# VectorE's program in a two-trip loop of three skippable parts, the first trip only branching over them

## The chip, the cores and the metric

One core of one Trainium2 chip. The time is the device time of one execution in microseconds; each kernel is run several times, and medians are quoted. The profile is of one execution; its times count from the start of the span, which is 1.8 us shorter than the device time of that same execution (294.18 us for the kernel before).

A ratio with an interval is the mean time of one kernel's fast runs over the mean time of the kernel before's fast runs in the same rounds, so it is not quite the ratio of the medians.

## The reference, cut to what matters

```python
h  = x + attention(layernorm(x), k_cache, v_cache, wq, wo)   # one token, B=2, 32 heads of 192,
                                                             # the last 2048 of 8192 positions
h2 = h + (gelu(layernorm(h) @ w_gate) * (layernorm(h) @ w_up)) @ w_down
```

Nearly all the work is reading: 122.29 MB of keys, values and weights, each byte used once.

## The kernel before: the parts that the change and the argument touch

The kernel records every operation in a list for its engine, with the semaphores it waits for, and then writes the lists out. TensorE's list is written as a four-trip loop; the other engines' lists are straight lines:

```python
    def emit(self, name, eng, sems, ops=None):
        for o in self.per.get(name, ()) if ops is None else ops:
            self.emit_one(o, eng, sems, [...])
    ...
        @block.vector
        def _(e):
            P.emit("dve", e, sems)
```

VectorE's list has 290 operations, 318 instructions when built: first some 55 that build constants (identity, masks, the normalised x), then the copies of transposed keys and the softmax of 16 groups, then the FFN's small steps.

All loads go through one queue into a ring of six slots of 24,576 bytes in each partition. A load is issued when what it overwrites has been read. The first four (k0, wq, k1, v0) need nothing; the fifth, k2, overwrites part of wq:

```python
K_AT = (0, SLOT, 3 * SLOT, 5 * SLOT)
V_AT = (2 * SLOT, 4 * SLOT)
WQ_AT = 3 * SLOT + SLOT // 2          # 2.5 slots long
...
        transposes(0, 0); transposes(0, 1)   # k0: TensorE, copied out by ScalarE and VectorE
        q_rows()                             # reads wq, then frees it: k2 may be issued
```

## Time and profile before

| | before |
|---|---|
| time, median (range) | 293.96 us (293.91 to 294.05) |
| span in the profile | 292.4 us |
| mean DMA rate over the span | 418 GB/s |
| busy share: TensorE, VectorE | 67%, 44% |
| VectorE's first operation | 1.10 us |
| packets of instructions on q14 in the span | 3 |

How to read it: the DMA engines are the bound, as the prediction shows with the profile's rows (one queue of data holds 97.9% of their time). The page counts 16 DMA engines, and the semaphore of each load is raised 16 times. I take that for 16 parts, one on each engine: wq has 128 pieces of 2.27 us, 8 of them make 18.1 us, and wq's first part landed 18.13 us after k0's. What waits for a load starts after the last of the 16: wq's came at 29.73 us, the query matmuls start at 29.87. The trace keeps the 16 times, though not which DMA engine is which. For the kernel before (us; the three latest of 16 in columns four to six):

```
load  issued   first   14th    15th    last     last behind first
k0      0.74   10.50   10.70   10.71   10.82    0.3
wq      1.42   28.63   28.83   28.92   29.73    1.1
v0      2.63   43.21   43.53   44.35   44.85    1.6
k2     35.65   50.53   50.83   51.67   52.15    1.6
k13   188.12  220.41  222.03  222.05  222.51    2.1
wd2   260.85  287.07  288.65  288.66  289.09    2.0
```

Even here a few parts are late, and the lateness hardly shrinks (0.1 us at most): the pieces of a load are of equal size and the DMA row stands at nine tenths or more from the fifth slice to the last but one, so a part that is 1.10 us behind in wq is still 1.14 behind in v0 and in k2, and 1.13 in k5.

The 16 landings also hint at what made them late, by the time at which each one falls behind. TensorE's packets on q8 (16,384 bytes) at 34.70, 51.09, 60.18, 77.56 and 92.17 us each put one more part 1.6 us behind: one part is so in k1, five are in k5. So TensorE's fetches fall on different parts. VectorE's two packets on q14, at 17.06 and 149.81, fit one and the same part: it is 1.1 behind from wq on (the second latest in v0) and 2.1 from v7 on.

### The profile page before, as it was taken

To read this page: it belongs to the slowest core of one execution; us is meant where nothing else is said; L and a number is where in the kernel's file an instruction comes from. 1 tells how busy PE (TensorE), PEld (TensorE's weight loads), DVE (VectorE), ACT (ScalarE), POOL (GpSimd) and SP (SyncE) were. 2 spreads that over 40 slices of the span, in tenths; PEclk is the share of its full clock that TensorE was granted. 3 is DMA by queue.
4 is the path that set the end of the run, shared out by engine and by line. 5 is a ranking of instruction groups with operands and counts; after the bars stand their busy time and mean duration, and the time that the engine had idled before them with its cause. 6 is when DMAs were issued, how large, how long until landed. Compare 5 with 4: busy or idle time off the path is not lost.

```text
span 292.4 us, 5066 instructions
## 1 busy us (share of the span) xinstructions
PE 196.2 (67%) x2141; PEld 151.6 (52%) x2141; DVE 128.2 (44%) x311; ACT 96.3 (33%) x120; POOL 8.6 (3%) x36
## 2 busy tenths in 40 slices
PE   2450769848677298849493597659596959585584
PEld 1440436728475285628281575456566657563242
DVE  5950075713447045525264155425265535352231
ACT  2150116623442143616161154325342525341000
POOL 4000020000000000000000000000000000000000
PEclk9996679995979579998899599969797968897755
DMA  7997999999999999999999999999999999999993
GB/s 269 430 531 338 433 447 436 430 433 430 423 408 448 430 434 428 430 430 430 430 402 450 434 430 430 430 430 434 430 430 430 430 430 434 430 430 405 425 416 148
DMA packets 6362, 122.44 MB, mean 419 GB/s; under 512 B 718, under 2 KB 848, under 8 KB 1360
## 3 DMA queue, kind: packets, MB, share of 16 engines
q1 hardware_dynamic: 6336, 122.29, 97.9%
q8 instruction: 7, 0.11, 0.2%
q14 instruction: 3, 0.02, 0.0%
q10 hardware_dynamic: 16, 0.01, 0.0%
HBM read 122.29 MB, written 0.00 MB: 418 GB/s over the span
## 4 chain that ended last, share of the span: by engine, by line
DMA 76%; PE 20%; SPq 2%; DVE 1%; issue 0%
DMA ring<-in_A_k_cache_dram 57%; PE tps L555 15%; DMA ring<-in_A_wq_dram 10%; DMA ring<-in_B_w_down_dram 10%; PE tps L576 2%; SPq L347 2%; PE ops L657 1%; PE m L708 1%; PE m L690 1%; DVE ktr L567 0%; DVE ering L408 0%; PE m L850 0%; PE m L641 0%; PE m L671 0%; DVE yrow L856 0%
## 5 line engine op out<-in xcount | busy, mean ns | idle before, releaser
L555 PE MATMUL tps<-identf,ring 128*128 128x128 f32 x768 | 114.4, 317 | 45.4 <-DMA ring<-in_A_k_cache_dram 44.1
L555 PEld LDWEIGHTS tps<-identf,ring 128*128 128x128 f32 x768 | 105.5, 166 | 48.4 <-DMA ring<-in_A_k_cache_dram 45.4
L564 ACT ACTIVATE ktr<-tps 128x1024 bf16<-128x1024 bf16 x80 | 79.4, 1023 | 84.0 <-PE tps L555 84.0
L567 DVE COPY ktr<-tps 128x1024 bf16<-128x1024 bf16 x112 | 74.0, 687 | 71.3 <-PE tps L555 70.4
L632 ACT ACTIVATE eexp<-sm,nm 128x512 bf16<-128x512 f32 x16 | 11.5, 721 | 64.1 <-DVE nm L630 64.1
L657 PE MATMUL ops<-ring,ering 128*32 128x384 bf16 x512 | 24.7, 337 | 4.8 <-DMA ring<-in_A_v_cache_dram 4.7
L613 PE MATMUL sps<-ktr,rq 128*16 128x512 bf16 x384 | 25.8, 403 | 1.1 <-POOL rq L408 1.1
L621 DVE CUSTOM_DVE_ANT_1 sm<-sps,mska 128x512 f32<-128x512 f32 x16 | 11.1, 692 | 34.9 <-PE sps L613 34.9
L657 PEld LDWEIGHTS ops<-ring,ering 128*32 128x32 bf16 x512 | 12.7, 98 | 13.3 <-DMA ring<-in_A_v_cache_dram 6.2
L613 PEld LDWEIGHTS sps<-ktr,rq 128*16 128x16 bf16 x384 | 9.5, 90 | 11.9 <-issue 2.1
L628 PEld LDWEIGHTS m<-mrhs,pm 128*128 128x128 bf16 x16 | 1.5, 96 | 22.8 <-DVE mrhs L404 22.8
L576 PE MATMUL tps<-ring,xnT 128*32 128x384 bf16 x80 | 5.7, 472 | 10.9 <-DMA ring<-in_A_wq_dram 10.9
L628 PE MATMUL m<-mrhs,pm 128*128 128x16 bf16 x16 | 2.9, 183 | 14.7 <-DVE mrhs L404 14.7
L408 POOL TENSOR_TENSOR rq<-qs,mask 128x96 bf16<-128x96 bf16 x16 | 5.6, 359 | 195.4 <-PE sps L613 161.3
L576 PEld LDWEIGHTS tps<-ring,xnT 128*32 128x32 bf16 x80 | 3.1, 134 | 13.4 <-issue 11.1
L599 DVE CAST qs<-ops 128x384 bf16<-128x384 f32 x1 | 0.6, 558 | 17.7 <-PE ops L594 17.7
L408 DVE TENSOR_TENSOR ering<-m,mask 128x256 bf16<-128x256 f32 x16 | 6.7, 419 | 3.2 <-PE m L641 3.2
L708 PE MATMUL m<-ring,ot 128*2 128x320 bf16 x96 | 4.7, 340 | 2.4 <-DMA ring<-in_A_wo_dram 2.4
L583 ACT ACTIVATE qrow<-tps 128x768 bf16<-128x768 f32 x1 | 0.8, 812 | 15.6 <-PE tps L576 15.6
L788 ACT ACTIVATE lnv<-tps,eps_t 98x1 f32<-98x1 f32 x1 | 0.3, 262 | 17.3 <-PE tps L786 17.3
L641 PE MATMUL m<-sel,eexp 128*128 128x64 bf16 x64 | 5.0, 206 | 1.2 <-ACT eexp L632 1.2
L641 PEld LDWEIGHTS m<-sel,eexp 128*128 128x128 bf16 x64 | 4.7, 111 | 1.7 <-DVE nm L630 1.3
(124 smaller groups left out, 88.8 us busy)
## 6 DMA issues: line engine op xcount, KB each, us to landing
ring<-in_A_k_cache_dram SPq DMA_DIRECT2D x16, 3072.0 KB, 31.2
ring<-in_A_v_cache_dram SPq DMA_DIRECT2D x16, 3072.0 KB, 27.3
ring<-in_A_wq_dram SPq DMA_DIRECT2D x1, 7680.0 KB, 28.3
ring<-in_A_wo_dram SPq DMA_DIRECT2D x4, 1920.0 KB, 21.5
ring<-in_B_w_gate_dram SPq DMA_DIRECT2D x1, 1920.0 KB, 31.5
ring<-in_B_w_up_dram SPq DMA_DIRECT2D x1, 1536.0 KB, 24.8
ring<-in_B_w_down_dram SPq DMA_DIRECT2D x1, 960.0 KB, 27.2
ring<-in_B_w_down_dram SPq DMA_DIRECT2D x1, 480.0 KB, 27.9
```

Source lines behind the costliest of these rows:

```text
L347: P.op("sp", lambda e, v=v, src=src: e.dma_start(v, src), W=toks + [("sem", sem)], dma=sem)
L408: return lambda e: e.tensor_tensor(out=out, in0=a, in1=b, op=op)
L555: ins = e.transpose(tps[bi][:, 128 * u:128 * (u + 1)], kv[:, off:off + 128], identf[:, :])
L564: act(lambda e, dst=dst, bv=bv: e.activation(out=dst, in_=bv, func=ACT.Copy), W=[("kt", n)], X=[("t", bi)])
L567: dve(lambda e, dst=dst, bv=bv: e.tensor_copy(dst, bv), W=[("kt", n)], X=[("t", bi)], cls=0)
L576: ins = e.matmul(tps[0][32 * r:32 * (r + 1), 0:384], lhsT=xnT[:, c, 32 * J:32 * (J + 1)], rhs=wq[:, c, 1536 * J + 384 * r:1536 * J + 384 * ...
L613: ins = e.matmul(sps[32 * ch:32 * ch + 16, :], lhsT=rq[:, g % 4, k, :], rhs=ktr[:, k // 2, 1024 * ch + k % 2:1024 * (ch + 1):2], start=(k ...
L621: dve(lambda e: e.tensor_tensor_reduce(out=sm[:, :].rearrange("p (u x) -> p u x", u=4), in0=sps[:, :].rearrange("p (u x) -> p u x", u=4), ...
L632: act(lambda e: e.activation(out=eexp[:, :], in_=sm[:, :], func=ACT.Exp, bias=nm[:, 0:1], scale=1.0, accum_out=zr[:, g % 4:g % 4 + 1]), R= ...
L641: ins = e.matmul(o, lhsT=eexp[:, 128 * u:128 * (u + 1)], rhs=sel64[:, :], start=True, stop=True)
L657: ins = e.matmul(ops_[32 * r:32 * (r + 1), 0:384], lhsT=ering[:, g % 4, t, :], rhs=vv[:, 384 * t:384 * (t + 1)], start=(g % 4 == 0 and t < 4),
L708: ins = e.matmul(m1[32 * r:32 * r + 2, 192:512], lhsT=ot[:, kk, :], rhs=wo[:, kk - k0, 320 * h:320 * (h + 1)], start=(kk == 1 or J < 2 and ...
```

## The change

Intent: let VectorE touch its whole program once at the start, so that its instructions are on the chip when they are needed.

```diff
+DVE_CUTS = (80, 200)
 ...
         @block.vector
         def _(e):
-            P.emit("dve", e, sems)
+            l = P.per["dve"]
+            with e.Fori(0, 2) as i:
+                for lo, hi in zip((0,) + DVE_CUTS, DVE_CUTS + (len(l),)):
+                    with e.If(i > 0):
+                        P.emit("dve", e, sems, l[lo:hi])
```

In the built program the branches stand at instruction 4, 86 and 218, and the loop's end at 321 and 322 of 325.

## The prediction

> **What bounds the kernel now.** I read the page's slices first, then the DMA queue's table, then the chain that ended last, then the timelines of TensorE and of the DMA-issuing engine at the start, where the change acts.

> The slices show the 16 DMA engines at nine tenths or more in nearly every slice, while VectorE is at four tenths on average:

> ```profile
> DVE  5950075713447045525264155425265535352231
> ...
> DMA  7997999999999999999999999999999999999993
> ```

> The queue table says that one queue of data holds 97.9% of the engines' time. The two rows marked "instruction" are the fetches of the engines' own programs, 7 and 3 in the whole span:

> ```profile
> q1 hardware_dynamic: 6336, 122.29, 97.9%
> q8 instruction: 7, 0.11, 0.2%
> q14 instruction: 3, 0.02, 0.0%
> ```

> The chain that ended last is 76% DMA and 1% VectorE. So the kernel is a stream of 122.29 MB at about 430 GB/s, and the question about any delay is whether it leaves that stream without work. The head of the chain in order of time (start, length, what) shows where it could:

> ```profile
> 1.42 28.31 DMA ring<-in_A_wq_dram
> 29.73 0.14 issue
> 29.87 5.76 PE tps L576 x61
> 35.64 0.02 issue
> 35.65 0.54 SPq L347
> ```

> Four loads are issued in the first 3.2 us (k0, wq, k1, v0). The fifth, k2, overwrites part of wq and is issued at 35.65, when the query matmuls (L576) have read wq. TensorE's timeline at the start (start, length, what, idle before):

> ```profile
> 3.75 0.35 PE L468 MATMUL m<-identb,xrow 2*128 2x2 bf16 x5 [3.75 <-DVE eps_t L439]
> ...
> 10.86 3.54 PE L555 MATMUL tps<-identf,ring 128*128 128x128 f32 x16 [4.26 <-DMA ring<-in_A_k_cache_dram]
> 15.07 3.89 PE L555 MATMUL tps<-identf,ring 128*128 128x128 f32 x32 [0.67 <-DVE ktr L567]
> 29.87 5.74 PE L576 MATMUL tps<-ring,xnT 128*32 128x384 bf16 x80 [10.91 <-DMA ring<-in_A_wq_dram]
> ```

> The k0 transposes end at 18.96, and TensorE then has nothing to do for **10.91 us** until wq has landed. VectorE feeds it three things before that: the identity (written by 3.43 us in VectorE's timeline), the normalised x (7.43) and the copies of the transposed k0, which stand behind 13 us of constant building (first copy 14.34).

> [...]the packets on q14 are 8,192 bytes[...]; TensorE's on q8 are 16,384. Two of q14's, at 17.05 and 149.81 us, fit VectorE[...] (59 and 179 of its instructions had started[...]).[...] In this trace TensorE's compare-and-branch records, which it already has in its four-trip loop, last 68 to 349 ns, and each of its three jumps back to the loop's top is followed by the next instruction within 0.3 us: there the target was still on the chip (no q8 fetch falls between 92 and 275 us).[...] the q14 fetch at 17.05 ran while wq moved (10.8 to 28.6 us), among its 61,440-byte pieces of 2.27 us each, not after them.

> **The change part by part.** Nothing is removed. No engine but VectorE has a different order, and VectorE executes the same operations with the same waits. Added on VectorE:

> - *Trip one.* Two register moves, three taken branches over the parts, one register add, one taken branch back. In the built program the branches stand at instruction 4, 86, 218 and about 322 of some 325. Branches alone, at TensorE's 0.07 to 0.35 us: 4 times 0.2 is 0.8 us. Fetches: with block borders near 61, 189 and 317 (from the two fetches above, a few instructions uncertain), the jump to 86 lands in the second block, which must be preloaded since the kernel before walks into it without a pause; the jump to 218 lands in the third[...]; the jump to 322 lands at or just beyond the fourth border; the jump back needs the first block, which may have been overwritten. That is one to three misses.
> - *Cost of a miss.* No row measures it. The nearest small transfer is xrow (2.5 KB): issued at 0.74, landed at 2.27, so 1.5 us; the output store took from 290.26 to 291.98, 1.7 us. With the 24,576-byte pieces of k0 in the way (0.91 us each) I estimate 2 to 3 us. So VectorE starts D = 0.8 + 2 x 2.2, about **5 us late**, between 2 and 10.
> - *Trip two.* Three branches not taken and the loop's end: under 1 us in all, spread over the run, and partly under waits for other engines (VectorE waits 70.4 us in total for the transposes alone).

> What of D reaches the end? With D = 5 the identity is there at 8.4, before k0 lands at 10.8. Constant building ends at 19.4 instead of 14.4, the k0 copies about 24.4, the transposes about 24, still 5 us before wq lands at 29.73. D costs nothing up to 10.9. Beyond that k2 would be issued late, but k1 and v0 are still queued at 35.65: the trace has v0's last semaphore at 44.85, so less some 1.5 us of start-up, another **7.5 us** pass before the stream runs dry. Only D over about 18 us costs time, and then one for one. In mid-run, loads are issued far ahead (one at 36.88 lands 29.88 us later, while its own 3,145,728 bytes at 430 GB/s need 7.3), so a stall of VectorE of a few us there is absorbed too. Sum: 293.94 + 0 at the start + 0 in the middle + about 0.1 for branches in the tail = **294.0 us**.

> **The rivals.** *A, a miss in the tail.* The last VectorE operations are moved some 5 instructions later, so that the fourth block's border may fall among them (the gelu at 284 to 288 us). There the slack is small: the last weights land at 289.09 and the matmuls ahead of them (L850) end at 288.93. If trip one spoils sequential prefetch, a miss there costs about 2 us: 296.[...] Against: 190 instructions stand ahead in straight order on trip two[...]. I give it one in ten. *B, fetches stuck behind whole packets.* [...]for k0 (8 pieces per engine, 7.3 us) and wq (18 us), two misses could take 25 us, D would pass 18 and the time go to 300 or more.[...] Against: it was still served inside wq. Three in a hundred. *C, faster.* Trip one could act as a warm-up that takes fetch stalls out of the run. But the waits of VectorE are all named after another engine's work, with no unexplained gap at 17 or 150 us, and VectorE does not bound the stream. One in a hundred.

> **Range and chances.** The centre is 294.0; the three runs before spread by 0.14 us. Low 293.4 for a rearrangement of the stream; high 296.2 for rival A. 2% is 5.9 us, which only rival B reaches: slower 0.03, faster 0.01, same 0.96.

> **What would show it.** VectorE's first operation starts about 5 us later than 1.10, and q14 shows two to four more fetches in the first 10 us (right), or none (the misses were not there, D about 1). TensorE's idle time before L576 shrinks from 10.91 to about 6 and is still ended by wq; L576 still starts near 29.87 and the fifth load near 35.65. From there every time in the chain agrees within 0.3 us. The prediction is wrong if L576 is released by VectorE, if the DMA row shows a dip near slice 6, or if VectorE has an unexplained gap after 284 us.

Passages are cut from this record where that is marked: they stated what no trace or run of this case shows. That a fetch waits for all pieces of a load on its DMA engine was B's assumption (the "whole packets" of its heading are these pieces; its 25 us are my estimate from 8 pieces of k0 at 0.91 us and 8 of wq at 2.27). In "it was still served inside wq" the fetch at 17.05 us is meant. The block borders near 61, 189 and 317, and with them the one to three misses, are an estimate from the two fetches at which 59 and 179 of VectorE's instructions had started, 120 apart; that the borders were set 128 apart was not shown by the trace.

## The result and the profile after

The changed kernel takes **299.11 us** (298.97 to 299.16) against 293.96: ratio 1.0174, interval 1.0156 to 1.0192. That is 5.15 us slower, within 2% but well outside the range of 293.4 to 296.2.

The page's slices and queue table of the changed kernel:

```profile
DVE  0006738563526335616237154434366425262231
...
DMA  7998989999999999999999999999999999999990
...
q1 hardware_dynamic: 6336, 122.29, 96.5%
q8 instruction: 7, 0.11, 0.2%
q14 instruction: 9, 0.07, 0.1%
```

VectorE does nothing in the first two slices and almost nothing in the third, and q14 has 9 packets instead of 3. Their share of the DMA engines' time is 0.1%, which looks like nothing. The data still moves in every slice, though slice 6 shows 8 tenths instead of 9, the dip that the prediction had named as a sign of being wrong.

VectorE's timeline (start, length, operation, idle before it):

```profile
21.74 0.23 DVE L436 CAST cf<-ci 128x128 f32<-128x128 int32 x1 [21.74 <-issue]
...
33.25 1.26 DVE L568 COPY ktr<-tps 128x1024 bf16<-128x1024 bf16 x2
```

Its first operation starts at 21.74 us, 20.6 later than before, and "issue" says that it waited for no other engine. TensorE's timeline:

```profile
25.38 3.65 PE L556 MATMUL tps<-identf,ring 128*128 128x128 f32 x16
33.98 5.56 PE L556 MATMUL tps<-identf,ring 128*128 128x128 f32 x32 [4.95 <-DVE ktr L568]
39.48 3.43 PE L577 MATMUL tps<-ring,xnT 128*32 128x384 bf16 x80
```

The query matmuls (here L577) start at 39.48 instead of 29.87, straight after the k0 transposes. The idle 10.91 us are used up. The chain that ended last, in order of time:

```profile
12.07 9.49 issue
...
33.98 5.56 PE tps L556 x32
39.55 3.39 PE tps L577 x80
42.95 0.54 SPq L348
...
44.24 26.62 DMA ring<-in_A_k_cache_dram
```

So k2 is issued at 42.95 instead of 35.65. From this chain the loss looks like VectorE's late start. But a chain only says that a load was issued at 44.24 and landed 26.62 us later, not why it took as long. The landings of the changed kernel:

```
load  issued   first   14th    15th    last     last behind first     last, against before
k0      0.74   10.49   10.70   10.74   12.33    1.8                   +1.5
wq      1.42   28.63   28.80   28.86   33.41    4.8                   +3.7
v0      2.63   43.25   43.39   43.44   48.96    5.7                   +4.1
k2     42.95   52.56   52.80   52.91   56.26    3.7                   +4.1
k13   192.68  222.40  224.11  224.12  227.05    4.7                   +4.5
wd2   265.42  289.03  290.71  290.72  293.60    4.6                   +4.5
```

Fifteen parts of wq land when they did before. **One part is 4.8 us late**, and stays late. By v0, which was issued at 2.63 us as before, 4.1 of the 5 us are already lost, and no load had yet been issued late. When k2 is late, the other fifteen DMA engines wait 2.0 us for it (50.53 becomes 52.56), but the late one does not: its k2 follows its v0 by 56.26 - 48.96 = 7.3 us, the ordinary time of a load (8 pieces of 0.91 us).

The packets on q14 fit. The trace has the times of the 8,192-byte packets of instructions in the span:

```
before   17.06                                      113.16  149.81
after     4.59  9.98  16.40  19.64  25.15  33.84    117.04  147.98  293.56
```

The one at 113 to 117 us I take for ScalarE's, since it came at 97.82 in the run delay_only below, where ScalarE has six instructions more. That leaves VectorE 2 before and 7 after; whose the last one is, 3.6 us before the end, the trace does not say. By v0 six fetches have put one part 5.7 us behind, 0.95 us each, though each packet itself took only 0.31 to 0.33 us.

How many instructions is such a packet, a block in what follows? At the kernel before's packets at 17.06 and 149.81 us, 59 and 179 of VectorE's instructions had started. In trip two of the changed kernel, counted in program order, it was 59 at 33.84, 178 at 147.98 and 320 at 293.56, if that one is VectorE's. From these counts, 119 to 142 apart, I estimate about 130 instructions to a block.

VectorE's own branch records tell the stall of each jump: jump to 218 at 1.56 us, next instruction at 6.37 (**4.8 us**); jump to 321, next at 11.91 (**5.5**); jump back to the top, next at 21.56 (**9.5**, with two fetches in it).

### The profile page after: what moved, and what is told of

Its sections match the earlier page's. It is cut to its first block, busy times and chain, and to the rows that moved or that the text cites. A ratio compares the mean times of both kernels' runs of the same rounds, so it can differ in the third digit from the quotient of the medians.

```text
span 297.2 us, 5079 instructions
## 1 busy us (share of the span) xinstructions
PE 192.5 (65%) x2141; PEld 149.0 (50%) x2141; DVE 126.4 (43%) x311; ACT 96.1 (32%) x120; POOL 8.5 (3%) x36
## 3 DMA queue, kind: packets, MB, share of 16 engines
q1 hardware_dynamic: 6336, 122.29, 96.5%
HBM read 122.29 MB, written 0.00 MB: 412 GB/s over the span
## 4 chain that ended last, share of the span: by engine, by line
DMA 65%; PE 21%; issue 8%; DVE 4%; SPq 2%; ACT 0%; DVEq 0%; ACTq 0%
DMA ring<-in_A_k_cache_dram 55%; PE tps L556 17%; DMA ring<-in_B_w_down_dram 10%; SPq L348 2%; PE tps L577 1%; PE ops L658 1%; DVE pg L405 1%; PE m L709 1%; PE m L691 1%; DVE ktr L568 0%; DVE ering L409 0%; PE m L642 0%; PE m L458 0%; PE m L450 0%; DVE orow L405 0%
## 5 line engine op out<-in xcount | busy, mean ns | idle before, releaser
L556 PE MATMUL tps<-identf,ring 128*128 128x128 f32 x768 | 113.0, 314 | 47.0 <-DMA ring<-in_A_k_cache_dram 41.4
L614 PE MATMUL sps<-ktr,rq 128*16 128x512 bf16 x384 | 24.7, 389 | 1.1 <-POOL rq L409 1.1
L436 DVE CAST cf<-ci 128x128 f32<-128x128 int32 x1 | 0.2, 227 | 21.7 <-issue 21.7
L709 PE MATMUL m<-ring,ot 128*2 128x320 bf16 x96 | 5.5, 381 | 1.6 <-DMA ring<-in_A_wo_dram 1.6
L409 DVE TENSOR_TENSOR orow<-m,wm 128x1536 bf16<-128x1536 f32 x3 | 5.2, 1750 | 0.0
```

Source lines behind the costliest of these rows:

```text
L409: return lambda e: e.tensor_tensor(out=out, in0=a, in1=b, op=op)
L556: ins = e.transpose(tps[bi][:, 128 * u:128 * (u + 1)], kv[:, off:off + 128], identf[:, :])
L614: ins = e.matmul(sps[32 * ch:32 * ch + 16, :], lhsT=rq[:, g % 4, k, :], rhs=ktr[:, k // 2, 1024 * ch + k % 2:1024 * (ch + 1):2], start=(k ...
L709: ins = e.matmul(m1[32 * r:32 * r + 2, 192:512], lhsT=ot[:, kk, :], rhs=wo[:, kk - k0, 320 * h:320 * (h + 1)], start=(kk == 1 or J < 2 and ...
```

## The experiments

Three theories. **LANE**: each instruction fetch holds up the one DMA engine that carries it by 0.7 to 1 us, all of such an engine's fetches go to the same one (VectorE's and GpSimd's; TensorE's do not, as seen above), and a load lands with its last part. **LATE**: VectorE's late start delays k2 and the stream runs dry. For the size of the start itself, **FOUR LINES**: VectorE keeps the last four blocks that it fetched and the changed kernel touches a fifth, against **JUMPS**: any jump back over some blocks fetches again.

| run | 8,192-byte packets in the span | VectorE's first op, us | last part of k13 behind first, us | time, us | ratio to before (interval) |
|---|---|---|---|---|---|
| before | 3 | 1.10 | 2.1 | 293.96 | |
| changed | 9 | 21.74 | 4.7 | 299.11 | 1.0174 (1.0156 to 1.0192) |
| delay_only | 4 | 21.94 | 1.7 | 296.88 | 1.0097 (1.0080 to 1.0114) |
| pool_jumps | 13 | 1.09 | 6.1 | 299.14 | 1.0170 (1.0153 to 1.0187) |
| loop_later | 4 | 1.10 | 2.9 | 295.04 | 1.0032 (1.0015 to 1.0049) |
| near_loop | 4 | 1.98 | 2.0 | 294.92 | 1.0032 (1.0015 to 1.0049) |
| three_blocks | 4 | 7.03 | 2.0 | 294.87 | 1.0029 (1.0012 to 1.0046) |
| one_part | 6 | 4.82 | 3.7 | 295.46 | 1.0045 (1.0029 to 1.0062) |
| loads_wait | 9 | 10.03 | 2.0 | 303.71 | one run |
| after_short | 3 | 7.13 | 2.0 | 294.25 | 1.0008 (0.9994 to 1.0022) |
| before_short | 3 | 1.10 | 1.9 | 293.98 | 1.0000 (0.9986 to 1.0014) |

All results were correct.

### delay_only: the late start without the fetches

```diff
+        for w in (4096,) * 5 + (1024,):     # ScalarE, idle here, 20 us
+            act(lambda e, w=w: e.activation(out=ktr[:, 0, 0:w], in_=dm[:, :].to_broadcast([128, w]), func=ACT.Copy), ...)
-        dve(lambda e: e.tensor_copy(cf[:, 0, :], ci[:, :]), R=["ci"], W=["cf0"])
+        dve(lambda e: e.tensor_copy(cf[:, 0, :], ci[:, :]), R=["ci", ("kt", 0)], W=["cf0"])
```

> VectorE's first operation waits for six idle ScalarE copies and so starts at about 21 us, as in the changed kernel (21.74), but its program is straight: no loop, no branch, no extra instruction fetch. Theory LANE (each instruction fetch holds up the one of 16 DMA engines that carries it by about 0.9 us, and a load has landed only when the last of its 16 parts has): almost all of the 5.15 us goes away; what is left is the 2.0 us by which the other 15 parts of k2 started late in the changed kernel, less the 0.5 to 1 us by which one part is late anyway: about 295.3, between 294.5 and 296. Theory LATE (VectorE's late start delays the issue of k2 and leaves the stream dry): the whole loss stays, about 299. In the landings of k2 the last of 16 parts is about 1 us behind the first (LANE), not 3.7.

Measured: 296.88 us, 2.80 over the kernel before of its rounds (294.08), a little above LANE's range and far from LATE's 299. k2 was issued at 43.70, still later than in the changed kernel, and its first part landed at 53.39, 2.9 us later than before, but its last part at 53.66, only 0.3 behind the first, against 56.26 in the changed kernel. A late start alone therefore costs 2.8 us, by the dry stream, and can't be the 5.15.

### pool_jumps: fetches on another engine, VectorE left alone

```diff
         @block.gpsimd
         def _(e):
-            P.emit("pool", e, sems)
+            l = P.per["pool"]
+            P.emit("pool", e, sems, l[:-16])
+            with e.Fori(0, 2) as i:
+                for k in range(2):
+                    with e.If(i > 0):
+                        for _k in range(260):
+                            e.memset(dm[:, 260 * k + _k:260 * k + _k + 1], 0.0)
+                with e.If(i < 1):
+                    P.emit("pool", e, sems, l[-16:])
```

> VectorE's program is that of the kernel before. GpSimd, idle from 3 to 38 us, jumps early over two stretches of 260 small memsets (about 4 extra fetches by 38 us) and runs through them after its last useful operation at 204 us (about 5 more fetches). VectorE and the issue of k2 are not delayed. LANE: each fetch costs the DMA engine that carries it 0.9 us; if one engine carries all of GpSimd's, the landings' last part slips by 3 to 4 us early and by 4 to 5 us more after 204 us, in all 299 to 302; if the fetches are spread over the engines, 294 to 295.5. LATE: 294 to 294.5 whatever the spread.

Measured: 299.14 us, ratio 1.0170, within LANE's range for one part carrying all, and as slow as the changed kernel, although VectorE's program is untouched and starts at 1.09. The slices of its page:

```profile
POOL 3000020000000000000000000000178500000000
...
q14 instruction: 13, 0.11, 0.1%
```

GpSimd runs through its memsets in slices 29 to 32 (211 to 235 us), where the trace has six packets, at 209.46 to 235.55. At k12, just before, one part was 3.2 us behind the first; at k14, just after, 7.2; the second latest stayed at 1.9. The six fetches cost that part 3.9 us, 0.65 each. The memsets are not to blame: in trip one, when GpSimd only jumps over them, four packets (of the five from 4.92 to 16.85 us, one is VectorE's) had already put one part of wq 3.2 us behind, 0.8 each, while the second latest, which fits VectorE's one fetch, was 0.9 behind. This is LANE, on another engine and at another time, with nothing late about VectorE. Ten extra fetches for an idle engine cost this kernel 5.06 us. That this equals the loss under study, where six packets were added, is chance.

### loop_later: the same kind of loop, begun where VectorE is idle

```diff
+            P.emit("dve", e, sems, l[:60])
+            with e.Fori(0, 2) as i:
+                for lo, hi in ((60, 200), (200, len(l))):
+                    with e.If(i > 0):
+                        P.emit("dve", e, sems, l[lo:hi])
```

> The same two-trip loop, but it begins only after VectorE's copies of the transposed k0 (60 operations in), with parts 60 to 200 and 200 to the end. The jumps fall where VectorE is idle anyway (19.4 to 37.1 us), so the issue of k2 should stay near 35.7 us. LANE: four extra fetches on VectorE's part of the DMA engines by 45 us, 4 x 0.9 = 3.6 us, so 297.0 to 298, and the last part of v0 lands about 3.5 us after the 15 others. LATE: no loss, 294 to 294.5.

Measured: 295.04 us, 0.96 over before (294.08), less than I expected of LANE and more than LATE allows. The reason for the miss is the number of fetches: I expected four extra, the trace has one (VectorE's at 23.73, 29.13 and 34.66). The last part of v0 was 2.9 us behind for three fetches. One extra fetch, 0.96 us: the price per fetch holds. What did not come is any refetch: after jumping from 31.17 us at the loop's end back to its top, VectorE's next instruction came at 31.48. That was the first sign that a jump back over two blocks is cheap, and led to FOUR LINES.

### near_loop: all the branches, no far target

```diff
+            with e.Fori(0, 2) as i:
+                for lo, hi in ((0, 15), (15, 30), (30, 45)):
+                    with e.If(i > 0):
+                        P.emit("dve", e, sems, l[lo:hi])
+            P.emit("dve", e, sems, l[45:])
```

> The two-trip loop with three skippable parts of 15 operations over VectorE's first 45 operations alone: the same number of branches as the changed kernel, but every target lies in the first block of instructions, which is on the chip. If the branches themselves cost time, VectorE starts several us late; if only fetches do, it starts 0.7 to 1.2 us late (seven branches and moves of about 0.1 us), no extra fetch is seen, and the time is that of before, 293.8 to 294.2.

Measured: VectorE starts 0.88 us late, as expected of branches alone, and no extra fetch comes early. But the time is 294.92, 0.84 over before, against 293.8 to 294.2 expected. The trace shows one more packet, at 285.82: the loop adds 7 instructions, and VectorE's 325 now pass a block border shortly before the end of the span, where the 318 of before reached it only after (293.52). The last part of wd2 is 2.8 us behind instead of 2.0. So even this miss is one fetch, 0.84 us, and the branches cost the kernel nothing that shows.

### three_blocks and one_part: how far trip one reaches

```diff
+                for lo, hi in ((0, 80), (80, 200), (200, 270)):     # three_blocks: 20 operations follow the loop
...
-DVE_CUTS = (80, 200)
+DVE_CUTS = ()                                                       # one_part: one jump from 4 to 319
```

> The changed kernel with one difference: the loop ends after operation 270 of 290, so that its end stands at instruction 298, in the third block[...], and trip one never enters the fourth. Theory FOUR LINES (VectorE keeps the last four blocks it fetched, and the jump back in the changed kernel is dear because entering the fourth block asks for a fifth, which overwrites the first): the jump back finds its block, trip one costs one miss of about 5 us, VectorE starts at about 7 us instead of 21.7, no block is fetched twice; the only extra fetch in the span is one at 282 to 287 us, where the 7 added instructions push the program over a block border before its end, as in near_loop: 294.9 within 0.3. Theory JUMPS (every far jump back refetches, only two blocks are held): VectorE starts after 15 us or later, four or more extra fetches, 297 to 299.

> The changed kernel without cuts: the loop's one part is skipped in one jump from instruction 4 to 319, over the second and third block. FOUR LINES: the jump fetches the fourth block and asks for a fifth; with the first two that makes four, so the jump back finds the first; VectorE starts at about 7 us, later the third is fetched: one extra fetch in the span, 0.9 us: 294.9 within 0.3. JUMPS: the jump back refetches the first block, start at 15 us or later, and blocks two to four again: 297 or more. LATE (only VectorE's start counts): 294.0.

three_blocks measured 294.87, as FOUR LINES said. VectorE's timeline begins

```profile
7.03 0.23 DVE L435 CAST cf<-ci 128x128 f32<-128x128 int32 x1 [7.03 <-issue]
```

and its jump back over two blocks, at 6.56, went on at 6.85: 0.29 us, without a fetch, so VectorE held at least three blocks. The packets on q14 are at 4.48, 9.88, 112.00 and 285.64: nothing is fetched twice, and the one extra is again the border near the end. The same three jumps over the parts, with the loop's end moved from instruction 321 to 297, cost 0.83 instead of 5.15 us.

one_part missed its 294.9 at 295.46, in the direction of more fetches: VectorE starts at 4.82, as cheap as FOUR LINES wants, the jump back is quick (4.36 to 4.65), but later two packets come, at 18.33 and 144.79, that the theory did not expect. It jumps over a whole block in between, which the others do not. So the jump back is as FOUR LINES says, but by what rule a block is asked for again stays open. The last part of k13 is 3.7 us behind for four fetches, and LANE holds once more.

### loads_wait: the price of a fetch without other traffic

```diff
-                P.op("sp", lambda e, v=v, src=src: e.dma_start(v, src), W=toks + [("sem", sem)], dma=sem)
+                P.op("sp", lambda e, v=v, src=src: e.dma_start(v, src), R=["cf0"] if key == ("k", 0) else [],
+                     W=toks + [("sem", sem)], dma=sem)     # k0 waits for VectorE's first operation
```

> The changed kernel, but the first load waits for VectorE's first operation, so that trip one's fetches meet no other traffic. If the 5 us of a miss is waiting behind pieces of k0 and wq on the DMA engine, the misses shrink from 4.9, 5.5 and 9.5 us to about 2, 2 and 4 and VectorE starts at 9 to 10 us; if it is the fetch's own latency, they stay and VectorE starts at 21 us. The total time is longer by the delay of the loads, about 303 to 315, and tells nothing else.

Measured: from jump to next instruction 2.3, 2.4 and 3.4 us, against 4.8, 5.5 and 9.5 with the loads running. VectorE starts at 10.03. So half and more of a miss is waiting in the traffic. The first load was issued at 10.29 instead of 0.74, 9.55 us later, and the span is 301.92 instead of 292.38, 9.54 longer: after that shift nothing else was lost, and the last part of k13 is 2.0 us behind, as in the kernel before. So the fetches of trip one, which met no loads here, cost no part anything.

### after_short and before_short: the whole program in the loop, nine instructions fewer

```diff
-DVE_CUTS = (80, 200)
+DVE_CUTS = (70, 190)
...
-        dve(lambda e: e.memset(eps_t[:, :], EPS), W=["eps"])
+        pool(lambda e: e.memset(eps_t[:, :], EPS), W=["eps"])
         # likewise onesd, xnT, lsx, ef and the five of ge; before_short is the kernel before with these alone
```

> The changed kernel, the whole of VectorE's program in the two-trip loop in three parts as before, but ten small constant-building operations moved to GpSimd and the cuts moved by ten with them, so that VectorE's program has 316 instructions instead of 325 and ends before the border of its fourth block (near 319). FOUR LINES and LANE: trip one never enters the fourth block, VectorE starts at about 7 us, no block is fetched twice, none is fetched at the end, in the span two blocks for VectorE as in the kernel before: 294.1 within 0.3, though 316 against 325 instructions is the only difference that matters. JUMPS or LATE: 297 to 299, since every jump of the changed kernel is still there.

> The control: the kernel before, no loop, with the same ten operations moved to GpSimd. Two fetches for VectorE in the span as before: 294.0 within 0.2 by LANE; if the move itself is worth something, it shows here and is to be taken off after_short.

after_short measured 294.25 (294.15 to 294.31), before_short 293.98, the kernel before in the same rounds 293.99. The loop with all its jumps now costs 0.27 us (the interval of its ratio includes 1), and moving the ten operations is worth nothing by itself. The queue table and TensorE's timeline of after_short:

```profile
q14 instruction: 3, 0.02, 0.0%
...
30.62 6.04 PE L577 MATMUL tps<-ring,xnT 128*32 128x384 bf16 x80 [6.54 <-DMA ring<-in_A_wq_dram]
```

Three packets as before, and the query matmuls wait for wq again, with 6.54 of the 10.91 us left: this is the picture that the prediction had drawn for the changed kernel. Nine instructions, which put the loop's end behind a block border, make the difference between it and 299.11.

No version beat the kernel before: the waits of VectorE there are all named after another engine's work, so there were no stalls for a warm-up to remove.

## Why the prediction was wrong

**What bounds the kernel** was right: the stream of loads. It failed in two steps, one that was mis-sized and one that was not in the sum.

**The size of D.** The prediction took "2 x 2.2" us for the misses and "D = 0.8 + 2 x 2.2, about 5 us, between 2 and 10". Measured: 20.6 us, 19.8 of them in three misses (4.8, 5.5, 9.5). The 2.2 was read from small transfers at moments when little else moved, and loads_wait shows it to be right for an idle queue (2.3 and 2.4); in the middle of k0 and wq it is 4.8 and more. I had put the load's pieces of 0.91 us into the estimate, but only one of them. The jump back was counted as a possible miss; it was one, with a second fetch before it.

**What D does** was nearly right. The prediction gave 10.9 + 7.5, "about 18 us", before the stream runs dry, and one for one beyond. delay_only, with 20.8, should then lose some 2.4; it lost 2.8. In the changed kernel fifteen of the sixteen parts of k2 are 2.0 us late, also as this rule has it. But the sum was right by luck, since two of its terms were off in opposite directions. The query matmuls, which are ready to start 9.6 us later, then took 3.5 us instead of 5.8 (the clock granted in them was 1.00 instead of 0.59), so that k2 was issued only 7.3 us later. And from there the stream had 7.3 - 2.0 = 5.3 us left, not 7.5: fourteen of v0's parts had landed by 43.53, 1.3 us before the last, and the start of k2 took more than the 1.5 us that was allowed (issued at 42.95, first part landed at 52.56, of which a load's ordinary 7.3 leaves 2.3).

**The missing term.** No line of the sum asks what a fetch costs the DMA engine that carries it. The prediction counted the packets on q14 and let them pass, and the table makes that easy: 0.1% of 16 engines' time. But one DMA engine seems to carry all of VectorE's, and it does not make up for it: in the changed kernel the last part is 4.7 us behind in k13 and still 4.6 in wd2. "Faster" and "slower" were weighed by whether VectorE's lateness reaches the stream (rival B), never by whether the fetches do. In v0 VectorE's part is 5.7 us behind with six fetches and was 1.1 behind with one: five more at 0.9 us. The last landing, which before was that of one of TensorE's parts, comes 4.1 us later; VectorE's fetch at 148 us adds 0.5. That fetches alone can do this is shown by pool_jumps, with VectorE on time; that the late start alone can't, by delay_only; and after_short, which keeps the loop, loses the repeated fetches and the late start together, and with them the time.

The two losses do not add up: the fifteen parts are 2.0 us late at k2 and the sixteenth 4.1, and the later one counts. That VectorE's lateness added nothing to the last part is read from the landings (7.3 us from v0 to k2); I have no run with the seven fetches and an early start. The sum closes: the last load of all, wd3, lands 4.8 us later than before, and the span is 4.80 longer. (wd2, just ahead, is 4.5 later; the ninth packet, at 293.56, falls between the two landings.) The times of the two profiled executions differ by 4.79; that the medians differ by 5.15 is the spread between executions, as the kernel before took 294.18 when it was profiled.

**Rival A**, a miss in the tail, did not occur: VectorE has no unexplained gap after 284 us in the changed kernel. **Rival B** came nearest: it had D over 18 us and a time of 300 or more, at three in a hundred. Half of what it assumed is there, since a miss takes about twice as long under load (4.8 and 5.5 us against 2.3 and 2.4 in loads_wait). But no fetch waited for a whole load: a part has 8 pieces of wq, 2.27 us each, and fetches ran among them at 16.40, 19.64 and 25.15 us, the first 4.3 us after the jump back at 12.07. And the last landing is late by the fetches and not by D. **The branches** were right: in near_loop trip one cost VectorE 0.88 us against 0.8 in the sum, with 0.2 us from one taken jump to the next. **Rival C** was rightly held to be nothing. That the time stayed within 2%, to which 0.96 was given, is luck too: nothing in the sum had a loss of 5 us.

Of the signs that I had named, one for being right came, two extra fetches on q14 in the first 10 us. The others failed: VectorE started 20.6 us late and not 5, the query matmuls' wait for wq was gone and they followed on VectorE's copies, k2 was issued at 42.95 and not near 35.65, and slice 6 of the DMA row has its dip.
